# Scores of own and preceding keys in one product, tanh for the first two groups' gates, the first mask on TensorE, and a new order of the work, in a windowed attention followed by a gated MLP

## The chip, the cores and the metric

The kernel runs on one core of one Trainium2 chip. The metric is the device time of one execution in microseconds. A run holds the span from the first to the last instruction and a little around it.

The engines named below are TensorE (PE: matmuls, and PEld: the loading of their stationary operand), VectorE (DVE), ScalarE (ACT), GpSimd (POOL), and SyncE (SP), whose queue and POOL's start the transfers (DMA). SBUF is the on-chip memory, PSUM the memory that matmuls write. Each engine works through its own list of instructions in order.

## What is computed

Attention over 768 positions with a window of 128 and 4 sink positions, for 4 sequences of 8 heads with 64 columns each; its output, 3072 tokens of 512, goes through an MLP of width 2048 with the gate h * sigmoid(1.702 h).

```python
scores = scale * np.matmul(q, k.transpose(0, 1, 3, 2))
keep = is_sink | in_window            # pos < 4, or 0 <= i - j < 128
scores = np.where(keep, scores, -1000000000.0)
scores = scores - np.max(scores, axis=-1, keepdims=True)
a = np.exp(scores)
a = a / (np.sum(a, axis=-1, keepdims=True) + 1e-09)
x = np.matmul(a, v)                   # heads side by side: 3072 x 512
h = x @ w_in                          # 512 x 2048
g = h * (1.0 / (1.0 + np.exp(-1.702 * h)))
out = g @ w_out                       # 2048 x 512
```

## The kernel before

**Blocks and groups.** The tokens are cut into 24 blocks of 128 (b; sequence bb = b // 6, place r = b % 6) for attention and 12 groups of two blocks (g) for the MLP. A block of queries meets its own 128 keys (own), the 128 keys ahead of it (prv, if r > 0) and the four sinks (snk, if r > 0). Since the window is 128 wide, for each query exactly one of a key position's own and preceding key is in the window, so own and preceding scores share one 128-wide tile: where the own key is later than the query, the preceding key's score is put in its place.

**Steps of a block.** POOL starts the loads of q, k and v, which also turn 32 bit floats into 16 bit ones (L253, L257). q and k are transposed to qkT: by TensorE and a copy for blocks 0 to 3 (tq, L336), by a DMA transpose from SP's queue for the others (L349). TensorE makes the scores, 8 products of 64 rows by 128 columns for own and 8 for prv (L374), and the sinks' (L390). VectorE puts prv's scores into own's tile by a predicated copy (L414), or, for r = 0, adds a mask (bias0, L406); takes the maximum of each head (L426, L442, L445), and subtracts it into e, an SBUF tile (L481, L496). ScalarE takes the exponential (a, L513); in blocks 0 to 3, one half is taken straight from PSUM by four activations with a bias (L467, set by nb). The weights a are transposed to at (ta on TensorE and a copy, L552, for blocks 0 to 3; a DMA transpose, L584, for others). POOL splits at by two selections into the part of the preceding keys, atp, and that of its own, at (L516, L520). TensorE multiplies by the values (av; sinks L603, own L609, preceding L613); each values tile has a 65th column of ones that gives the sum of the weights. VectorE divides by it (rcp and xn, L624 and L625; a "norm" below). xn is transposed to xT (tx, L638, and a copy for blocks 0 to 3; a DMA transpose, L649, for others).

**Sink values.** vsb holds the sinks' values of a sequence, 32 rows of 4 sinks x 8 heads, of which each head's columns are kept by a mask (ownm, L301), in a tile of 128 rows that is set to zero first (L235). It is multiplied by a ninth 128-wide piece of at.

**Steps of a group.** hT is made in 8 tiles of 8 matmuls of 128x256 (L669; group 0 is "split": 16 of 128x128, each for one block's tokens, so that it can begin with block 0 alone). ScalarE takes Gelu_apprx_sigmoid of each into gT (L681). Its table is another than the exponential's, so the planner batches the gates of a group, and a table load stands ahead of each change. The second product o takes 16 matmuls of 128x512 for each block, in four quarters (L697); a copy takes it to osb and SP's queue writes it out (L714).

**The order.** All steps are ops of a small planner (class Plan). Each op has an engine or a choice of two, a key (its urgency), a cost, ops it depends on, and PSUM or SBUF tiles that it takes and gives back (Buf, RING: how many of each ring there are). run() goes through time and lets each engine take, of the ops that are ready by its costs, the one with the smallest key; the resulting order is what each engine is given. On the chip each engine keeps that order and waits where something isn't there yet. Loads that aren't in the list `loads` have a time ahead of which the planner doesn't start them (after0, after).

**PSUM** has 8 banks of 2 KB a partition: mm 3 (hT, o, transposes, and the scores of own for blocks 1 and 3), own 2, pv 2 (prv and av), mi 1 (snk).

Of the kernel before, what the change touches and what calls it, by code (L numbers as in the profile page):

```python
# [27 lines left out]
    tq=(0, 1, 2, 3), ta=(0, 1, 2, 3), tx=(0, 1, 2, 3), nb={0: 1, 1: 1, 2: 1, 3: 1}, wide=(1, 3),  # L28
    split=(0,), gbatch=8, after0=25.0, after=8.0,
    loads="q0 k0 q1 k1 v0 v1 i0 i1 q2 k2 q3 k3 i2 i3 v2 v3 o0 o1 o2 o3".split(),  # L30
)
RING = dict(qkn=4, qkt=8, e32=4, a16=4, at=4, atp=4, xn=3, xt=4, gt=3, osb=4, mm=3, own=2, pv=2, mi=1)
# [15 lines left out]
class Op:  # L48
    def __init__(self, eng, key, cost, emit, deps=(), take=(), give=(), table=None, lat=0.2, xfer=0.0, after=0.0, batch=0, xt=False):
        self.eng = eng if isinstance(eng, dict) else {eng: cost}  # L50
        self.key, self.emit = key, emit
        self.deps = [d for d in deps if d is not None]
        self.take, self.give, self.table, self.batch = list(take), list(give), table, batch
        self.lat, self.xfer, self.after, self.xt = lat, xfer, after, xt
        self.start = self.end = self.done = None
        for b in self.give:
            b.left += 1


class Plan:  # L60
# [3 lines left out]
    def __init__(self, rings):  # L64
        self.ops, self.free = [], dict(rings)

    def add(self, *a, **kw):
        op = Op(*a, **kw)
        op.seq = len(self.ops)
# [3 lines left out]
    def _give(self, op):  # L73
        for b in op.give:
            b.left -= 1
            b.t = max(getattr(b, "t", 0.0), op.done)
            if b.left == 0:
                self.gives.append((b.t, b.ring))

    def run(self):  # L80
        t_eng = {e: 1.0 for e in self.ENGINES}
        free, table, batch, now = dict(self.free), "exp", 0, 0.0
        pending, order, self.gives = list(self.ops), [], []
        queue = {POOL: [], SP: []}
        lanes = {POOL: [], SP: []}
        while pending or any(queue.values()):
            for item in [x for x in self.gives if x[0] <= now]:
                self.gives.remove(item)
                free[item[1]] += 1
            for e in self.ENGINES:  # L90
                if t_eng[e] > now:
                    continue
                best = None
                for op in pending:
                    if e not in op.eng or op.after > now:
                        continue
                    if any(d.done is None or d.done > now for d in op.deps):
                        continue
                    need = {}
                    for b in op.take:  # L100
                        need[b.ring] = need.get(b.ring, 0) + 1
                    if any(free[r] < n for r, n in need.items()):
# [3 lines left out]
                    if op.xfer and len(lanes[e]) >= self.LANES:  # L106
                        d = lanes[e][-self.LANES].done
                        if d is None or d > now:
                            continue
                    if best is None or (op.key, op.seq) < (best.key, best.seq):  # L110
                        best = op
                if best is None:
                    continue
                op, cost = best, best.eng[e]
                op.on = e
# [5 lines left out]
                op.start, op.end = now, now + cost  # L121
                t_eng[e] = op.end
                for b in op.take:
                    free[b.ring] -= 1
# [3 lines left out]
                else:  # L128
                    op.done = op.end + op.lat
                    self._give(op)  # L130
                pending.remove(op)
                order.append(op)
            live = [q[0] for q in queue.values() if q and q[0][0].end <= now]
            times = [t for t in t_eng.values() if t > now] + [x[0] for x in self.gives if x[0] > now]
            times += [op.done for op in order[-400:] if op.done is not None and op.done > now]
            times += [op.after for op in pending if op.after > now]
            times += [now + h[1] * len(live) for h in live]
            assert times, [(o.eng, o.key) for o in pending[:20]]
            step = max(min(times), now + 1e-6) - now
# [3 lines left out]
            for h in live:  # L143
                if h[1] <= 1e-6:
                    queue[h[0].on].pop(0)
                    h[0].done = now + (0.6 if h[0].xt else 1.9)
                    self._give(h[0])
# [4 lines left out]
def _consts():  # L152
# [5 lines left out]
    own = np.zeros((32, 2, 4, D1), np.float16)  # L158
    for h in range(8):
        own[4 * h : 4 * h + 4, h % 2, h // 2] = 1.0  # L160
# [5 lines left out]
        own.reshape(32, 8 * D1),  # L166
# [4 lines left out]
def kernel(  # L171
# [39 lines left out]
    ident = const.tile([P, P], FP16, name="ident")  # L211
    later = const.tile([P, P], U16, name="later")
    bias0 = const.tile([P, P], BF16, name="bias0")
    bias1 = const.tile([P, 4], BF16, name="bias1")
    ownm = const.tile([32, 8 * D1], FP16, name="ownm")
# [4 lines left out]
    vsa = const.tile([32, 4, D1], FP32, name="vsa")  # L220
    vsb = const.tile([P, 4, 2, 4, D1], FP16, name="vsb")
# [3 lines left out]
    def hw(key, cost, fn, xfer, **kw):  # L225
# [7 lines left out]

    z_k = plan.add(DVE, -90, 0.2, lambda: nc.vector.memset(ksb, 0.0))
    z_v = plan.add(DVE, -89, 1.2, lambda: nc.vector.memset(vsb, 0.0))  # L235
# [3 lines left out]
        plan.add(DVE, -86 + i, 0.2, lambda i=i: nc.vector.memset(a16s[i][:, 8 * P : 9 * P], 0.0))  # L239
        for i in range(RING["a16"])  # L240
    ]
# [45 lines left out]
    for b in range(NBLK):  # L287
        for w in "qkv":
            if f"{w}{b}" not in ld:
                ld[f"{w}{b}"] = load_block(w, b, -60 + 8 * (b - 4), CFG["after0"] + CFG["after"] * nblk)  # L290
                nblk += w == "v"
    ld_win, ld_wout = [ld[f"i{f}"] for f in range(4)], [ld[f"o{f}"] for f in range(4)]

    o_vsa = [
        hw(-94 + bb, 0.45, lambda bb=bb: nc.sync.dma_start(vsa[:, bb, 0:D], v[bb, :, 0:4, :]), 0.1, deps=[z_s])
        for bb in range(Bsz)
    ]

    def vs_build(bb):
        def go(e):  # L300
            (nc.vector if e == DVE else nc.gpsimd).tensor_tensor(  # L301
                out=vsb[0:32, bb].rearrange("p l j d -> p (l j) d"),
                in0=vsa[:, bb].unsqueeze(1).to_broadcast((32, 8, D1)),
                in1=ownm.rearrange("p (n d) -> p n d", d=D1),
                op=ALU.mult,
            )

        return plan.add({DVE: 0.45, POOL: 0.8}, 48 * bb - 41, 0, go, deps=[o_vsa[bb], z_v, o_own])

    o_vsb = [vs_build(bb) for bb in range(Bsz)]  # L310

    def copy(e, dst, src):
        if e == DVE:
            nc.vector.tensor_copy(out=dst, in_=src)
        else:
# [3 lines left out]
    qkt = [sb("qkt", (P, 8, P), FP16, f"qkT{b}") for b in range(NBLK)]  # L319
    xt = [sb("xt", (P, 4, 2 * P), FP16, f"xT{g}") for g in range(NG)]  # L320
    o_qkt, o_ks, o_own_s, o_x = {}, {}, {}, {}

    for b in range(NBLK):
        bb, r = divmod(b, 6)
        g, i = divmod(b, 2)
        K0 = 8 * b
        nb = CFG["nb"].get(b, 0)


        if b in CFG["tq"]:  # L330
            tp = ps("mm", (P, 8, P), FP16, f"tq{b}")

            def t_qk(b=b, g=g, i=i, tp=tp):
# [5 lines left out]
                PE, K0 - 48, 0.55, t_qk, deps=[ld[f"q{b}"], ld[f"k{b}"], o_ident], take=[tp],  # L339
# [3 lines left out]
                {DVE: 0.65, ACT: 1.05}, K0 - 48, 0,  # L343
                lambda e, b=b, tp=tp: copy(e, qkt[b](), tp()), deps=[a], take=[qkt[b]], give=[tp],
            )
        else:

            def t_qk(b=b, g=g, i=i):
                nc.sync.dma_start_transpose(qkt[b](), qkn[g]()[:, i].rearrange("p w h d -> p (w h d)"))  # L349

            o_qkt[b] = plan.add(
                SP, K0 - 48, 1.25, t_qk, deps=[ld[f"q{b}"], ld[f"k{b}"]], take=[qkt[b]], give=[qkn[g]], xfer=1.26, xt=True
            )
        if r == 0:

            def sink_keys(b=b, bb=bb):
# [400 lines left out]
```

## Time and profile before

| what | us |
| --- | --- |
| median of 3 runs (252.06 to 254.63) | 253.05 |
| profiled execution | 252.76 |
| its span, first to last instruction | 251.0 |
| the first hT tile of group 0 starts at | 25.14 |
| the first hT tile of group 1 starts at | 58.97 |
| the last copy osb starts at | 247.11 |
| 12 + 12 table loads of 1.28 each | 30.8 |

The mean granted clock of TensorE was 0.976. The largest groups of the profile:

```profile
L669 PE MATMUL hT<-xT,w_in 128*128 128x256 f16 (+1 forms) x832 | 94.1, 268 | 3.8 <-ACT xT L316 1.3
L697 PE MATMUL o<-w_out,gT 128*128 128x512 f16 x384 | 86.2, 379 | 0.0
L681 ACT ACTIVATE gT<-hT 128x512 f16<-128x512 f32 x96 | 57.0, 597 | 45.3 <-PE hT L669 45.1
L414 DVE COPY_PREDICATED own<-later,prv 128x512 f32<-128x512 uint16 x40 | 25.9, 691 | 36.7 <-PE prv L374 29.0
L426 DVE TENSOR_REDUCE mx<-own 128x4 f32<-128x512 f32 x48 | 31.2, 681 | 0.1
```

A row is: line, engine, operation, tiles (output <- inputs), partitions x elements and type, count | busy us, mean ns of one | idle time of the engine just ahead of them, and what ended most of it. A matmul's mean is longer than the distance to the next, since they are pipelined: 8 of 128x256 take 0.87 us in a dense stretch, 4 of 128x512 take 0.87 as well. The page has four DMA rows that matter below:

```profile
w_out<-in_moe_w_out_dram POOLq DMA_DIRECT2D x4, 512.0 KB, 14.1
qkT<-qkn SPq DMA_TRANSPOSE x20, 4.9
at<-a SPq DMA_TRANSPOSE x20, 3.3
xT<-xn SPq DMA_TRANSPOSE x20, 5.7
```

The last number is the median time from issue to landing.

### The profile page before, as it was taken

The numbers are of one execution on the slowest core, as the hardware profiler recorded it, in microseconds if no ns is written. First come the engines' busy times: TensorE is split into PE (matmuls) and PEld (weight loads), VectorE is DVE, ScalarE is ACT, GpSimd is POOL, SyncE is SP. The second block draws the span as 40 slices with busy tenths as digits, with TensorE's granted clock in tenths as the row PEclk, the third lists the DMA queues.
The fourth block names the chain that finished last, engine by engine and source line by source line (L and its number), as shares of the span: only waits on it lengthen the run. The fifth ranks groups of instructions, "written<-read, shape, count | busy, mean of one in ns | idle before, by whom it ended". The sixth has DMA issues, their size and how long they took to land.

```text
span 251.0 us, 5308 instructions
## 1 busy us (share of the span) xinstructions
PE 217.1 (86%) x2123; PEld 148.1 (59%) x2123; DVE 133.7 (53%) x332; ACT 136.9 (55%) x198; POOL 113.5 (45%) x130
## 2 busy tenths in 40 slices
PE   0528787857998989998999996999999999999993
PEld 0306655434764845946747845848669477594851
DVE  4596920496687356964866556749647663010000
ACT  2326576825473474586466654657765666471621
POOL 8955832387471904904916807719055060210000
PEclk9999999985899999999999999999999999999998
DMA  9999999995999998999999999999999343320202
GB/s 77 167 175 193 206 188 151 156 129 82 136 110 190 169 149 201 101 117 202 156 159 231 127 111 215 110 175 182 119 253 130 71 131 44 74 77 3 84 0 84
DMA packets 138663, 34.09 MB, mean 136 GB/s; under 512 B 131440, under 2 KB 135568, under 8 KB 138640
## 3 DMA queue, kind: packets, MB, share of 16 engines
q0 software_dynamic: 79104, 13.64, 81.9%
q1 hardware_dynamic: 59536, 20.13, 44.0%
q8 instruction: 16, 0.26, 0.4%
q14 instruction: 7, 0.06, 0.1%
HBM read 27.43 MB, written 6.29 MB: 134 GB/s over the span
## 4 chain that ended last, share of the span: by engine, by line
PE 60%; DMA 20%; DVE 12%; issue 2%; POOL 2%; SPq 1%; ACT 1%; POOLq 0%; ACTq 0%; DVEq 0%
PE hT L669 27%; PE o L697 22%; DMA qkT<-qkn 8%; DMA qkn<-in_k_dram 5%; DMA at<-a 2%; DVE own L414 2%; PE own L374 2%; DMA xT<-xn 2%; DVE xn L625 2%; DVE mx L426 2%; DMA vsa<-in_v_dram 2%; PE av L609 2%; PE av L613 1%; DVE e L481 1%; PE prv L374 1%
## 5 line engine op out<-in xcount | busy, mean ns | idle before, releaser
L669 PE MATMUL hT<-xT,w_in 128*128 128x256 f16 (+1 forms) x832 | 94.1, 268 | 3.8 <-ACT xT L316 1.3
L697 PE MATMUL o<-w_out,gT 128*128 128x512 f16 x384 | 86.2, 379 | 0.0
L669 PEld LDWEIGHTS <-w_in 128*128 128x128 f16 x832 | 75.0, 99 | 14.6 <-issue 3.2
L681 ACT ACTIVATE gT<-hT 128x512 f16<-128x512 f32 x96 | 57.0, 597 | 45.3 <-PE hT L669 45.1
L516 POOL TENSOR_SCALAR_AFFINE_SELECT atp<-at 128x1024 f16<-128x1024 f16 (+1 forms) x23 | 22.5, 976 | 95.3 <-DMA at<-a 73.3
L697 PEld LDWEIGHTS <-gT 128*128 128x128 f16 x384 | 36.5, 98 | 41.0
L414 DVE COPY_PREDICATED own<-later,prv 128x512 f32<-128x512 uint16 x40 | 25.9, 691 | 36.7 <-PE prv L374 29.0
L426 DVE TENSOR_REDUCE mx<-own 128x4 f32<-128x512 f32 x48 | 31.2, 681 | 0.1
L316 ACT COPY osb<-o 128x512 f32<-128x512 f32 x23 | 13.5, 585 | 30.4 <-PE o L697 27.3
L513 ACT ACTIVATE a<-e 128x1056 f16<-128x1056 f32 (+3 forms) x27 | 24.3, 919 | 10.4 <-issue 8.8
L481 DVE TENSOR_TENSOR e<-own,mx 128x512 f32<-128x512 f32 x44 | 28.8, 683 | 1.2
L253 POOL DMA_DIRECT2D v<-in_v_dram x24 | 21.7, 906 | 4.6 <-DMA w_in<-in_moe_w_in_dram 3.0
L520 POOL TENSOR_SCALAR_AFFINE_SELECT at<-at 128x1024 f16<-128x1024 f16 (+1 forms) x23 | 22.4, 972 | 1.6
L257 POOL DMA_DIRECT2D qkn<-in_q_dram x24 | 21.9, 912 | 2.4 <-DMA w_out<-in_moe_w_out_dram 1.6
L257 POOL DMA_DIRECT2D qkn<-in_k_dram x24 | 21.7, 905 | 1.8 <-DMA w_out<-in_moe_w_out_dram 1.7
L625 DVE TENSOR_TENSOR xn<-av,rcp 128x256 f16<-128x256 f32 x48 | 20.4, 424 | 1.6
L609 PE MATMUL av<-v,at 128*128 128x65 f16 x192 | 17.5, 198 | 3.1 <-POOL at L520 2.9
L624 DVE RECIPROCAL rcp<-av 128x4 f32<-128x4 f32 x48 | 8.4, 174 | 21.6 <-PE av L613 20.0
L609 PEld LDWEIGHTS <-at 128*128 128x128 f16 x192 | 14.5, 100 | 5.9 <-POOL at L520 4.9
L374 PEld LDWEIGHTS <-qkT 64*128 64x128 f16 x352 | 11.0, 99 | 11.7 <-issue 6.4
L681 ACT ACT_TABLE_LOAD x12 | 15.4, 1283 | 0.2
L613 PE MATMUL av<-v,atp 128*128 128x65 f16 x160 | 15.3, 196 | 0.0
(43 smaller groups left out, 135.7 us busy)
## 6 DMA issues: line engine op xcount, KB each, us to landing
out_dram<-osb SPq DMA_DIRECT2D x24, 256.0 KB, 2.4
qkn<-in_q_dram POOLq DMA_DIRECT2D x24, 128.0 KB, 4.8
qkn<-in_k_dram POOLq DMA_DIRECT2D x24, 128.0 KB, 6.1
v<-in_v_dram POOLq DMA_DIRECT2D x24, 128.0 KB, 6.6
w_in<-in_moe_w_in_dram POOLq DMA_DIRECT2D x4, 512.0 KB, 10.3
w_out<-in_moe_w_out_dram POOLq DMA_DIRECT2D x4, 512.0 KB, 14.1
qkT<-qkn SPq DMA_TRANSPOSE x20, 4.9
at<-a SPq DMA_TRANSPOSE x20, 3.3
```

Source lines behind the costliest of these rows:

```text
L257: key, 0.88, lambda: nc.gpsimd.dma_start(buf()[:, i, w], src), 0.87,
L414: nc.vector.copy_predicated(out=own[l](), mask=later.unsqueeze(1).to_broadcast((P, 4, P)), data=prv[l]())
L426: lambda l=l, own=own, small=small: nc.vector.tensor_reduce(out=small[:, l], in_=own[l](), axis=AX.X, op=ALU.max),
L481: nc.vector.tensor_tensor(out=e32()[:, 512 * l : 512 * l + 512].rearrange("p (j s) -> p j s", j=4), in0=own[l](), in1=small[:, l].unsqueez ...
L513: nc.scalar.activation(out=a16()[:, lo:hi], in_=e32()[:, lo:hi], func=AF.Exp, scale=scale)
L516: nc.gpsimd.affine_select(out=atp()[:, lo : lo + n], in_=at()[:, lo : lo + n], pattern=[[0, n], [-1, P]], compare_op=ALU.is_gt, fill=0.0, ...
L520: nc.gpsimd.affine_select(out=at()[:, lo : lo + n], in_=at()[:, lo : lo + n], pattern=[[0, n], [1, P]], compare_op=ALU.is_ge, fill=0.0, ba ...
L609: nc.tensor.matmul(av()[:, j], at()[:, c], v65[:, b, h], start=(r == 0), stop=(r == 0))
L625: nc.vector.tensor_tensor(out=xn().rearrange("p (j l) d -> p l j d", l=2)[:, l], in0=av()[:, :, 0:D], in1=rcp.unsqueeze(2).to_broadcast((P ...
L669: nc.tensor.matmul(ht()[:, n], w_in16[:, c, bass.ts(f, P)], xt[g]()[:, c, tok], start=(c == 0), stop=(c == 3))
L681: lambda fs=fs, tok=tok, gt=gt, ht=ht: nc.scalar.activation(out=gt()[:, fs[0] : fs[-1] + 1, tok], in_=ht(), func=AF.Gelu_apprx_sigmoid),
L697: nc.tensor.matmul(po(), gt()[:, F, bass.ts(t, P)], w_out16[:, F], start=(F == 0), stop=(F == NF - 1))
```

## The change

- **Scores.** The transposed queries and keys of a sequence's six blocks lie in one tile, qs (128 x 6 x 8 x 128, two of them), so a block's keys and its predecessor's lie one behind the other and one product of 256 columns gives both. The score tile sc (two banks, two of them) holds two pairs of heads for preceding and own keys; a block has two such halves (u = 0, 1: heads 0 to 3 and 4 to 7), and maxima, subtractions and norms go by these halves. The predicated copy reads and writes the same tile.
- **First mask.** For r = 0 the mask is added by TensorE: per half two products of identb (the identity in bfloat16) with bias0, 256 columns each, ahead of the score products, which accumulate on it. The VectorE adds go.
- **Sinks.** Their scores snk are copied to an SBUF tile ss (VectorE or ScalarE; for r = 1 with the mask). vsb has 48 rows (0 to 15 for heads 0 to 3, 32 to 47 for 4 to 7); the product takes 16 rows. vsa is loaded by 8 transfers instead of 4. The large memset goes; small ones for e come.
- **Exponentials.** nb is empty: in all blocks both halves go through e on VectorE.
- **Gates of groups 0 and 1.** tanh(0.851 h) on ScalarE into th (32 bit, SBUF), then (th + 1) * h on VectorE into gT, which is twice the gate; the factor 0.5 goes into the copy of o to osb. Tanh is planned as of the exponential's table.
- **PSUM.** mm 3, sc 2 x 2, av 1 (values and snk).
- **Order.** q, k and v of blocks 4 and 5 are in the list `loads`; the planner's costs are new; and each op's key is replaced by a number of the list KEYS (some 1010 numbers), a permutation. An engine's order within the program so differs throughout: hT tiles, o quarters and halves of blocks come interleaved, and hT tiles of two groups too.

The core of the diff:

```diff
-    tq=(0, 1, 2, 3), ta=(0, 1, 2, 3), tx=(0, 1, 2, 3), nb={0: 1, 1: 1, 2: 1, 3: 1}, wide=(1, 3),
-    split=(0,), gbatch=8, after0=25.0, after=8.0,
-    loads="q0 k0 q1 k1 v0 v1 i0 i1 q2 k2 q3 k3 i2 i3 v2 v3 o0 o1 o2 o3".split(),
...
+    nb={},
...
+    tanh=(0, 1),
...
+    loads="q0 k0 q1 k1 v0 v1 i0 i1 q2 k2 q3 k3 i2 i3 v2 v3 q4 k4 q5 k5 o0 o1 o2 o3 v4 v5".split(),
...
-RING = dict(qkn=4, qkt=8, e32=4, a16=4, at=4, atp=4, xn=3, xt=4, gt=3, osb=4, mm=3, own=2, pv=2, mi=1)
+RING = dict(qkn=4, qs=2, e32=4, a16=4, at=4, atp=4, xn=3, xt=4, gt=3, osb=4, th=2, mm=3, sc=2, av=1)
...
+    def sink_values(bb):
+        def load(u):
+            nc.sync.dma_start(vsa[32 * u : 32 * u + 16, bb, 0:D], v[bb, 4 * u : 4 * u + 4, 0:4, :])
...
+        sc = [ps("sc", (P, 2, 2, 2, P), FP32, f"sc{b}_{u}") for u in range(2)]
+
+        def scores(u, bb=bb, r=r, sc=sc):
+            t = sc[u]()
+            if r == 0:
+                for l in range(2):
+                    nc.tensor.matmul(
+                        t[:, l, :, 1], identb, bias0.unsqueeze(1).to_broadcast((P, 2, P)), start=True, stop=False
+                    )
+            for jj in range(2):
+                for l in range(2):
+                    rows, j = slice(64 * l, 64 * l + 64), 2 * u + jj
+                    if r == 0:
+                        nc.tensor.matmul(
+                            t[:, l, jj, 1], qs[bb]()[rows, r, j], qs[bb]()[rows, r, 4 + j], start=False, stop=jj == 1
+                        )
+                    else:
+                        nc.tensor.matmul(
+                            t[:, l, jj], qs[bb]()[rows, r, j], qs[bb]()[rows, r - 1 : r + 1, 4 + j],
+                            start=True, stop=True,
+                        )
...
+                    nc.vector.copy_predicated(
+                        out=t[:, :, 1], mask=later.unsqueeze(1).to_broadcast((P, 4, P)), data=t[:, :, 0]
+                    )
...
                 if r > 0:
+                    rows = slice(32 * u, 32 * u + 16)
                     nc.tensor.matmul(
-                        av().rearrange("p j d -> p (j d)"), at()[:, 8],
-                        vsb[:, bb, l].rearrange("p j d -> p (j d)"), start=True, stop=False,
+                        av().rearrange("p n d -> p (n d)"), at()[rows, 8],
+                        vsb[rows, bb].rearrange("p n d -> p (n d)"), start=True, stop=False,
                     )
...
+            if g in CFG["tanh"]:
+                th = sb("th", (P, 4 * P), FP32, f"th{g}_{u}")
...
+                        out=th(), in_=ht().rearrange("p f t -> p (f t)"), func=AF.Tanh, scale=0.851
...
+                    lambda fs=fs, tok=tok, gt=gt, ht=ht, th=th: nc.vector.scalar_tensor_tensor(
+                        out=gt()[:, fs[0] : fs[-1] + 1, tok], in0=th().rearrange("p (f t) -> p f t", f=len(fs)),
+                        scalar=1.0, in1=ht(), op0=ALU.add, op1=ALU.mult,
+                    ),
...
+    if KEYS:
+        for op, key in zip(plan.ops, KEYS):
+            op.key = key
     order = plan.run()
```

## The prediction

> **What bounds the kernel now.** I read the page first, then the order of the matmuls and the idle time ahead of them on TensorE, then the other engines where TensorE was thin, then windows with the granted clock, then the landing times of the transposes.
>
> The page, engines and slices (one digit is 6.3 us):
>
> ```profile
> span 251.0 us, 5308 instructions
> ...
> PE 217.1 (86%) x2123; PEld 148.1 (59%) x2123; DVE 133.7 (53%) x332; ACT 136.9 (55%) x198; POOL 113.5 (45%) x130
> ...
> PE   0528787857998989998999996999999999999993
> ```
>
> TensorE is full from the tenth digit on; what is lost lies in the first 59 us. The first 8-matmul hT tile of group 1 starts at 58.97, the last o matmul ends at 247.1: 188.1 us in which only TensorE sets the pace. Up to 58.97 it is fed by attention of blocks 0 to 5 and by group 0. The timelines of VectorE and ScalarE say why that takes so long:
>
> ```profile
> 33.08 0.18 DVE L496 TENSOR_TENSOR e<-snk,mx 128x32 f32<-128x32 f32 x1
> 47.30 0.56 DVE L314 COPY at<-ta 128x512 f16<-128x512 f16 x2 [14.04 <-PE ta L552]
> ...
> 36.78 1.28 ACT L681 ACT_TABLE_LOAD   x1
> ...
> 44.13 1.28 ACT L513 ACT_TABLE_LOAD   x1
> 45.43 0.75 ACT L513 ACTIVATE a<-e 128x512 f16<-128x512 f32 x2
> ```
>
> VectorE stands 14.04 us for the transposed weights of blocks 2 and 3: their scores are ready at 33.1, but ScalarE holds the gate table until group 0 is through and takes the exponentials only at 45.4. The windows then show the clock:
>
> ```profile
> 56.00:59.00 3.00, 0.99 (x12) 0.67 (x10) 2.86 (x9) 0.58 (x1) 1.09 (x1) 0.50 0.87 165
> 59.00:62.00 3.00, 3.00 (x29) 1.99 (x29) 0.94 (x3) 2.53 (x3) 2.99 (x4) 0.50 0.12 10
> ```
>
> The columns are window, length, busy PE, PEld, DVE, ACT, POOL, granted clock, DMA share, GB/s. After the thin stretch the clock is at 0.50, and stays so to about 64.7: of 5.7 us of dense work half, 2.85 us, is lost.
>
> **The sum's base.** The profiled execution took 252.76 us, 1.76 outside its span of 251.0; it lies 0.3 below the median of the runs, 253.05. All terms below are against 252.76.
>
> **Group 1 starts earlier.** In the changed program group 0 and 1 take tanh, which follows exponentials with no table load between (table loads fall from 24 to 16), so blocks 2 and 3 no longer wait for the gates. What is then next is VectorE. From the first maximum of block 0 to the last xn of block 3 its order holds 40 operations of 128x512 (12 maxima, 10 selections, 10 subtractions, 8 tanh gates), 8 norms and some 40 small ones. In dense stretches of the trace a large one follows the next after 0.60 us (two selections at 24.91, the next at 26.10), a norm takes 0.55, small ones 0.1 to 0.35: 24.0 + 4.4 + 6.7 = 35.1 us. The gate reads an SBUF and a PSUM operand of 512 floats; its nearest row is the subtraction, so 0.60. The chain begins at 11.2 instead of 14.0: the two bias adds (1.30) are gone from VectorE and the small loads of sink values, of which the last lands at 11.3 now, are split among the maxima. That gives 46.3 if VectorE never waits. I add 4: block 4's scores need its transposed queries. Now 46 units of 131 KB (14 loads of q, k and v, 8 weight loads of four units) land between 4.3 and 38.9, 0.75 each; in the new order of POOL's queue 36 units stand up to the last query of blocks 4 and 5, so it lands at about 31, and a transpose took 3.0 to 7.5; and three o quarters (0.87 each) stand ahead of block 5's scores on TensorE. With tx and the xT copy (0.4 + 0.6) group 1 starts at 51.0, bounds 47.2 (no wait) and 55 (the transpose at 7.5 and one more such wait): **-8.0** (-11.8 to -4.0).
>
> **Clock.** In the new stretch from 23 to 51 TensorE has about 18 us of work in 28 (before: 5 in the 12 us ahead of 59). I take the clock as held: **-2.85**, or 0 if not (251.3 in the end): between 47 and 59 no gap on TensorE was above 1.34 us and yet the clock fell, so thin work is enough, and the new stretch is only twice as dense. The Trainium skill ("TensorE: Matmul & The Clock Gate", Part 1) lets the clock fall only after an idle window of about 3.4 us. By that rule the loss would not return; the trace does not agree with it, and decides.
>
> **TensorE's own work after that.** One o quarter of group 0 now stands behind the first hT of group 1: **+0.9**. The mask by TensorE is 16 products of 256 columns; 12 of them, for blocks 6, 12 and 18, fall in the dense part, at 0.109 each (hT row, 0.87 for 8): **+1.3**; what it takes off VectorE there (6 adds of 0.6) lies beside it and gives nothing. The merged score product halves the matmuls but not their columns: 8 x 128 now take 0.33 as own and 0.22 as prv just behind it; 8 x 256 as two halves take 0.44 plus what own pays for coming after other work, 0.11, once or twice: 0.55 to 0.66 against 0.55, or less by the saved issues. I take 0, bounds -1.5 and +1.7 for 15 blocks. The sink values' product takes 16 rows instead of 128 in each of 34 dense halves; no row shows it. It costs nothing if like the 128-row product (0.11 for 260 columns, no gap), 0.11 if like a change to 64 rows, 0.22 if it pays on the way back as well: 0 to 7.5. The rest of the half keeps 128 rows, so I take 0.05: **+1.7**. The Trainium skill ("TensorEngine Tiling (Array Packing)", Key Properties) says that a change of tiling mode drains the engine, which speaks against this part; at own's 0.11 each half it would make 250.4 in place of 248.4, within the forecast's band.
>
> **New waits in the dense part.** Before, from 58.97 on, 88 hT tiles and 88 o quarters at 0.87 and 25 us of attention make 178.3 us of work; 188.1 - 178.3 - 2.85 leaves 7.0 of waits and switches. Among these only one is for xT:
>
> ```profile
> 73.38 5.65 DMA xT<-xn
> 79.07 1.05 PE hT L669 x8
> ```
>
> From group 3 on the old order leaves 9.7 to 14.4 us of TensorE work between a group's last values product and its first hT. The new order, counted in the same units (hT tile 0.87, o quarter 0.87, score half 0.22, sinks 0.19, values half 0.36), leaves 4.7, 6.2, 6.6, 3.6, 5.8, 6.2, 5.8 for groups 2 to 8, 13.2 for 9, 4.3 and 4.4 for the last two. Group 5, for one: two hT, one o quarter, one values half, two score halves, sinks. The hand-over needs a norm (0.66 from matmul to xn), 0.1, the transpose and 0.05:
>
> ```profile
> DMA to landing us min/median/max: 2.4/5.7/8.4
> ```
>
> At the median that is 6.5, and 1.8 + 0.3 + 0 + 2.9 + 0.7 + 0.3 + 0.7 = 6.7 us are uncovered; the last two groups run after the loads, where it landed in 2.4 to 3.5, and are covered. TensorE waits in order, so all that is queued behind that hT waits too. A single bank for values and sinks, and shorter ways from scores to values (8.5 to 14.3 us of other work for six of blocks 4 to 10, before 10.8 to 24.3; one values half waited 2.1 for POOL, one 1.1 and one 0.9 us went to transposed queries), I put at 3: together 9.7 in place of 7.0, **+2.7**. Bounds: 2.7 (all covered but these) and far above, below.
>
> Costed at nothing, since TensorE is the bound: 16 tanh gates' second pass on VectorE (group 1 with blocks 6 and 7 needs about 15 of 17 us there; without that cover 0.6 each), half-wise maxima, sink copies, eight small loads on SP's queue (0.7 each, done before block 4's transposes), the factor 0.5 in osb's copy, fewer table loads.
>
> Sum: -8.0 - 2.85 + 0.9 + 1.3 + 1.7 + 2.7 = -4.3, so **248.4**.
>
> **Rivals.**
> Covers hold: the transposes, issued singly, land near 3 as the late ones do; waits fall from 9.7 to about 2.7: 241.4. For it: 2.4 to 3.5 late. Against: none that I could resolve between 70 and 185 landed under 5.4.
> The gain is spent: the hand-over takes the mean of those (5.8, 5.6, 7.0, 7.2, 8.4, 5.7, 6.0, 5.4, 5.4, 8.1: 6.5); each of seven groups loses 0.8 more, 253.9; or the clock falls again, 251.3.
> Slower: the hand-over of xT becomes the bound at seven groups. At the upper half of those rows (7.7) uncovered time is 20.6 instead of 6.7: 262.3. It decides from a mean landing of 6.7, where waits pass 255.6. For it: the mean is close. Against: half of the rows are at 5.4 to 5.8.
> That the merged product saves TensorE time is not in the sum at all: equal columns.
>
> **Numbers.** Forecast 0.38 (244 to 250.5), covers hold 0.20 (below 244), gain spent 0.24, slower 0.18. A measurement here tells about 1% from no change (250.5 to 255.6): faster 0.58, same 0.24, slower 0.18. Range 241 to 258, leaving about 0.1 at each end; it takes in the bounds of the start and of the 16-row product.
>
> **What will show it.** VectorE without a 14 us gap and group 1's first hT near 51; granted clock 1.00 around 50 to 65; xT waits ahead of the first hT of groups 2, 5 and 6, near 2, 3 and 1 us; values halves still 0.36 to 0.41; 16 table loads. Wrong if group 1 starts after 55, or if TensorE waits more than 15 us after it.

## The result and the profile after

| | before | changed |
| --- | --- | --- |
| median us (range; runs) | 253.49 (252.06 to 254.63; 4) | 260.69 (260.38 to 261.03; 4) |
| profiled execution; its span | 252.76; 251.0 | 261.03; 259.3 |
| mean granted clock | 0.976 | 0.974 |
| first hT of group 0; of group 1 | 25.14; 58.97 | 23.73; 53.71 |
| last product starts | 246.65 | 254.44 |

The ratio is 1.0287, interval 1.0229 to 1.0345: slower, outside the range of the prediction. (Now and then a run is disturbed by a lower clock; ratios here leave such runs out and medians don't, so the two can differ, and one kernel below has no ratio.) The page of the changed kernel, engines, slices of 6.5 us and clock:

```profile
span 259.3 us, 5051 instructions
...
PE 230.3 (89%) x1979; PEld 142.9 (55%) x1979; DVE 149.6 (58%) x394; ACT 125.1 (48%) x184; POOL 113.8 (44%) x130
...
PE   0559695999959999999699999997999999999993
...
PEclk9999996799989999999979999999999999999999
```

TensorE is fuller than before (89% for 86%), with fewer matmuls, and yet later. The 14.04 us for which VectorE stood are gone: ScalarE takes tanh and exponentials in turn, with no table load between them. Its timeline:

```profile
32.80 0.60 ACT L765 ACTIVATE th<-hT 128x512 f32<-128x512 f32 x1 [1.14 <-PE hT L751]
33.92 0.78 ACT L600 ACTIVATE a<-e 128x512 f16<-128x512 f32 x2 [0.53 <-DVE e L562]
34.60 0.58 ACT L765 ACTIVATE th<-hT 128x512 f32<-128x512 f32 x1
```

What took the place of that gap is in TensorE's timeline and in the windows (columns as in the prediction, the clock third from the end):

```profile
41.78 0.27 PE L470 MATMUL snk<-ksb,qs 128*128 128x8 f16 x4 [2.60 <-DMA qs<-qkn]
...
43.71 4.94 PE L797 MATMUL o<-w_out,gT 128*128 128x512 f16 x12
48.48 0.24 PE L470 MATMUL snk<-ksb,qs 128*128 128x8 f16 x4
```

```profile
36.00:40.00 4.00, 2.84 (x45) 2.42 (x42) 2.75 (x7) 2.87 (x6) 2.82 (x5) 1.00 1.55 136
40.00:44.00 4.00, 2.22 (x22) 1.29 (x23) 1.91 (x4) 0.19 (x1) 2.93 (x4) 0.66 1.36 179
44.00:47.00 3.00, 3.00 (x8) 1.06 (x7) 2.97 (x11) 0.00 (x0) 0.86 (x2) 0.50 1.98 163
47.00:50.00 3.00, 3.00 (x19) 1.17 (x19) 1.23 (x4) 1.20 (x2) 0.29 (x1) 0.81 2.43 155
```

TensorE waits 2.60 us for block 4's transposed queries; then the clock is at half, and 12 o products take 4.77 us, which is 2.60 at 0.217 each.

**Where the time went.** From group 1's first hT to the last product I took, for every matmul, the distance to the start of the next, and set against it what its shape has in dense stretches (0.217 us for 512 columns on 128 rows, 0.109 for 256, half as much on 64 rows, where two run side by side). What is above that is a change of row count, a half clock (the distance doubled), or a wait (over 0.18).

| us | before | changed | difference |
| --- | --- | --- | --- |
| group 1's first hT at | 58.97 | 53.71 | -5.3 |
| products by their shapes | 173.9 | 175.9 | +2.0 |
| changes to 16 rows and back | 0 | 6.9 | +6.9 |
| changes to 64 rows and back | 4.1 | 6.3 | +2.2 |
| waits | 6.8 | 7.9 | +1.1 |
| half clock | 2.7 | 3.2 | +0.5 |
| rest | 0.1 | 0.3 | +0.2 |

With 0.5 more behind the last product's start this is the 8.3 us of the spans within 0.2. The largest term can be read in the timelines. A values half of the kernel before, then of the changed one:

```profile
101.82 1.04 PE L669 MATMUL hT<-xT,w_in 128*128 128x256 f16 x8
102.69 0.27 PE L603 MATMUL av<-vsb,at 128*128 128x260 f16 x1
102.80 0.19 PE L609 MATMUL av<-v,at 128*128 128x65 f16 x1
...
103.05 1.04 PE L669 MATMUL hT<-xT,w_in 128*128 128x256 f16 x8
```

```profile
97.76 0.49 PE L751 MATMUL hT<-xT,w_in 128*128 128x256 f16 x3
98.18 0.28 PE L688 MATMUL av<-vsb,at 16*128 16x260 f16 x1
98.39 0.20 PE L694 MATMUL av<-v,at 128*128 128x65 f16 x1
...
98.65 1.91 PE L751 MATMUL hT<-xT,w_in 128*128 128x256 f16 x16
```

Starts count, not lengths. Before, 8 hT take 0.87 and the product of 260 columns 0.11. After, 3 hT take 0.42 (0.33 by shape) ahead of the 16 rows, and the same 260 columns 0.21: about 0.10 going in and 0.10 coming out, and a half that is 0.47 long in place of 0.36.

### The profile page after: what moved, and what is told of

It reads as the page before. It is cut to its first block, busy times and chain, and to the rows that moved or that the text cites. A ratio compares the mean times of both kernels' runs of the same rounds, so it can differ in the third digit from the quotient of the medians.

```text
span 259.3 us, 5051 instructions
## 1 busy us (share of the span) xinstructions
PE 230.3 (89%) x1979; PEld 142.9 (55%) x1979; DVE 149.6 (58%) x394; ACT 125.1 (48%) x184; POOL 113.8 (44%) x130
## 4 chain that ended last, share of the span: by engine, by line
PE 67%; DMA 20%; POOL 7%; DVE 1%; ACT 1%; SPq 1%; issue 1%; POOLq 0%; ACTq 0%
PE o L797 28%; PE hT L751 28%; DMA qs<-qkn 6%; DMA qkn<-in_q_dram 6%; DMA xT<-xn 5%; POOL qkn L315 3%; PE sc L451 3%; PE av L694 3%; DMA at<-a 3%; PE av L688 2%; PE av L696 1%; POOL v L311 1%; POOL w_in L324 1%; POOL atp L603 1%; SPq L668 1%
## 5 line engine op out<-in xcount | busy, mean ns | idle before, releaser
L797 PE MATMUL o<-w_out,gT 128*128 128x512 f16 x384 | 94.6, 391 | 0.0
L781 ACT ACTIVATE gT<-hT 128x512 f16<-128x512 f32 x80 | 47.2, 597 | 39.0 <-PE hT L751 38.8
L511 DVE COPY_PREDICATED sc<-later,sc 128x512 f32<-128x512 uint16 x40 | 27.0, 690 | 16.8 <-PE sc L451 16.7
L600 ACT ACTIVATE a<-e 128x1088 f16<-128x1088 f32 (+3 forms) x31 | 27.2, 896 | 11.8 <-DVE e L562 7.0
L520 DVE TENSOR_REDUCE mx<-sc 128x4 f32<-128x512 f32 x48 | 32.2, 685 | 0.8 <-PE sc L447 0.4
L562 DVE TENSOR_TENSOR e<-sc,mx 128x512 f32<-128x512 f32 x48 | 32.3, 686 | 0.5
L382 ACT COPY osb<-o 128x512 f32<-128x512 f32 x18 | 10.6, 586 | 31.6 <-PE o L797 26.1
L451 PE MATMUL sc<-qs 64*128 64x256 f16 x160 | 15.9, 293 | 7.0 <-DVE e L562 5.5
L694 PEld LDWEIGHTS <-at 128*128 128x128 f16 x192 | 12.8, 99 | 8.0 <-DVE ss L478 1.5
L765 ACT ACTIVATE th<-hT 128x512 f32<-128x512 f32 x16 | 9.5, 594 | 13.4 <-PE hT L751 13.2
```

Of the source, the lines that this page charges most:

```text
L451: nc.tensor.matmul(t[:, l, jj], qs[bb]()[rows, r, j], qs[bb]()[rows, r - 1 : r + 1, 4 + j], start=True, stop=True,)
L511: nc.vector.copy_predicated(out=t[:, :, 1], mask=later.unsqueeze(1).to_broadcast((P, 4, P)), data=t[:, :, 0])
L520: lambda u=u, sc=sc, small=small: nc.vector.tensor_reduce(out=small[:, u], in_=sc[u]().rearrange("p l j w s -> p (l j) w s")[:, :, 1], axi ...
L562: nc.vector.tensor_tensor(out=e32()[:, 512 * u : 512 * u + 512].rearrange("p (j l s) -> p l j s", l=2, s=P), in0=sc[u]()[:, :, :, 1], in1= ...
L600: nc.scalar.activation(out=a16()[:, lo:hi], in_=e32()[:, lo:hi], func=AF.Exp, scale=scale)
L694: nc.tensor.matmul(av()[:, n], at()[:, h], v65[:, b, h], start=(r == 0), stop=(r == 0))
```

## The experiments

Ratios are to the kernel before on the same chip.

**The price of a row count.** The changed kernel with 128 rows, and the kernel before with 32:

```diff
-    vsb = const.tile([48, 4, 4, D1], FP16, name="vsb")
+    vsb = const.tile([P, 4, 2, 4, D1], FP16, name="vsb")
...
-                        av().rearrange("p n d -> p (n d)"), at()[rows, 8],
-                        vsb[rows, bb].rearrange("p n d -> p (n d)"), start=True, stop=False,
+                        av().rearrange("p n d -> p (n d)"), at()[:, 8],
+                        vsb[:, bb, u].rearrange("p n d -> p (n d)"), start=True, stop=False,
```

> The changed kernel with one thing altered: the sink product works on all 128 rows of the transposed weights against a table of own values that is zero outside its 16 rows, so that no product on 16 rows is left on TensorE; two builds of 16 rows per sequence replace one of 48. The output stays the reference's. Theory A (each change of the row count costs TensorE about 0.1 us, into the 16 rows and out of them, and 6.9 us of the changed kernel's trace are that): 34 halves lose about 0.2 us each, so the time falls from 260.7 to about 254 (252 to 256); in the trace the distances at the sink products lose their extra 0.1 us on either side. Rival B (the 0.1 us are waits of TensorE for the transposed weights that fall at the same place, or the loss lies in the order): the time stays at 259.5 to 261.5 and the idle time moves to another instruction. Where the expected time is missed upwards, rival C: the saved time is taken up by new waits for xT or for score tiles, which the list of waits would show.

```diff
-                        av().rearrange("p j d -> p (j d)"), at()[:, 8],
-                        vsb[:, bb, l].rearrange("p j d -> p (j d)"), start=True, stop=False,
+                        av().rearrange("p j d -> p (j d)"), at()[0:32, 8],
+                        vsb[0:32, bb, l].rearrange("p j d -> p (j d)"), start=True, stop=False,
```

> The kernel before with one thing altered: its sink product works on the 32 rows that hold own keys instead of on all 128; the output stays the reference's, and the order of instructions is the same. Theory A: a sink product on fewer rows costs about 0.1 us going in and 0.1 us going out, so 40 of them add 6 to 8 us: about 260 (257 to 262). Rival B (a product on few rows costs what its columns cost): the time stays within 1 us of the kernel before, 252 to 254.5.

Measured: 258.83 (254.8 to 260.55), ratio 1.0114 (0.9997 to 1.0231), so about 1.7% or 4.4 us below the changed kernel's ratio (its interval is wide and meets the changed kernel's; the medians differ by 1.9, the profiled spans by 3.4); and 257.16 (255.49 to 257.95), ratio 1.0143 (1.0069 to 1.0217). The second kernel's timeline has the same half as above:

```profile
103.53 1.03 PE L669 MATMUL hT<-xT,w_in 128*128 128x256 f16 x8
104.49 0.28 PE L603 MATMUL av<-vsb,at 32*128 32x260 f16 x1
104.71 0.20 PE L609 MATMUL av<-v,at 128*128 128x65 f16 x1
...
104.96 1.03 PE L669 MATMUL hT<-xT,w_in 128*128 128x256 f16 x8
```

0.96 for 0.87 ahead of it, 0.22 for 0.11, 0.47 for 0.36, by this one edit: 34 halves pay 3.3 going in (0.097 each) and 3.4 coming out (0.101). Theory A holds for the price; rival B falls in the trace. But 6.7 us more in the kernel before cost 3.6 us of time. In its profiled run the part from group 1 on took only 1.0 more, with 5.1 us less of waits (1.7 for 6.8) and 1.0 less of half clock, while group 1 came 3.7 later (62.64), with the clock low ahead of it. And 6.2 us less in the changed one (6.9, less 0.7 that score halves then pay on their way back) gave 4.4, with 4.4 more of waits (12.3 for 7.9). Block 0's first maximum came later there, at 13.83 in place of 12.40, but group 1 1.1 earlier, at 52.58, so it is not the start that took the gain. Rival C took part of it. The longest wait, in the chain of waits of the run with 128 rows:

```profile
124.28 0.43 DVE xn L711
124.71 0.02 issue
124.73 7.09 DMA xT<-xn
131.82 0.04 issue
131.86 1.14 PE hT L756 x9
```

In the changed kernel the same hand-over reads:

```profile
123.54 0.44 DVE xn L706
123.98 0.02 issue
123.99 6.03 DMA xT<-xn
130.03 0.04 issue
130.07 2.08 PE hT L751 x9
```

TensorE's work that covers it, from the last values product ahead of it to the wait, is the same in both within 0.1 us (4.1 and 4.2). What grew is the landing, from 6.03 to 7.09; why is open.

**What tanh is worth.** In the kernel before, with its own way of ordering:

```diff
-    split=(0,), gbatch=8, after0=25.0, after=8.0,
+    split=(0,), tanh=(0, 1), gbatch=8, after0=25.0, after=8.0,
```

> The kernel before with one part of the change alone: the gates of groups 0 and 1 by tanh (one ACT operation with the exponential's table and one on VectorE, the factor 0.5 at the output copies), everything else and its way of ordering as before. The output stays the reference's. Theory A (the 14 us gap ahead of group 1 came from the gate table's batch, and its end is worth what group 1 gains): group 1's first hT moves from 58.97 to 51 to 54, the end follows by 4 to 6 us: 247 to 250. Rival B (what group 1 gains is spent in later waits, for xT and q, k tiles, as in the changed kernel where the waits rose by 1.1 us and half-clock time by 1.2): 251 to 254. Slower than 254.6 would mean that the two extra operations per gate on VectorE and ACT are late for someone.

Measured: 256.71 (255.69 to 258.12), ratio 1.0137 (1.0064 to 1.0211). Both theories were too low; the time lies in the expectation's last branch, over 254.6. TensorE's timeline from the end of group 1 on:

```profile
67.37 0.40 PE L378 MATMUL own<-qkT 64*128 64x128 f16 x8
...
74.52 0.23 PE L378 MATMUL prv<-qkT,qkT 64*128 64x128 f16 x1 [0.74 <-DMA qkT<-qkn]
...
76.88 0.26 PE L378 MATMUL own<-qkT 64*128 64x128 f16 x1 [1.52 <-DVE e L485]
...
84.64 1.67 PE L673 MATMUL hT<-xT,w_in 128*128 128x256 f16 x7 [1.29 <-DMA xT<-xn]
```

Group 1 began at 51.02, as theory A had it, and is through its last o product at 71.4. Then there is nothing but attention until group 2's first hT at 84.64, which in the kernel before came at 79.07. From 78 to 86 the clock was at 0.50. MLP work that is done early is missing later as cover: that is one reading. The other is the expectation's, that the gates' second pass comes late for someone: VectorE was busy 13.1 of the 16 us from 70 to 86, and the wait at 76.88 ends on its subtraction. No run parts the two.

**The start of the changed kernel.** The searched order has the builds of all four sequences' vsb in VectorE's first microseconds; it stood for their loads until 9.79 us, and block 0's first maximum came at 12.40. They were moved to where they are needed:

```diff
     order = plan.run()
+    for build, op in zip(o_vsb, behind):
+        build.on = DVE
+        order.remove(build)
+        order.insert(order.index(op) + 1, build)
```

> The changed kernel with one thing moved: the four builds of the own values vsb (one per sequence) stand on VectorE directly behind the last subtraction of their own sequence's second block, in place of the first microseconds, where the searched order had them with those of sequences 2 and 3 ahead of block 0's first maximum; every other instruction keeps its place. The output stays the reference's. Theory C (part of the gain at the start is lost because VectorE stands until 9.79 and 10.89 us for the loads of vsa of sequences that are needed only after 100 us): block 0's first maximum moves from 12.40 to about 9.5, the first hT from 23.7 to about 21, group 1 from 53.7 to 51, and the time falls by 2 to 3 us to 258 to 259. Rival D (the start is bound by the loads of block 4's queries and keys, whose transposition landed at 41.7 us): all moves until then, but TensorE then waits longer for that landing, group 1 stays at 53 to 54 and the time at 260 to 261.

> The changed kernel with both: the sink product on 128 rows, and the builds of vsb moved to the second block of their sequence. (The run with 128 rows alone had its builds in the first microseconds too, twice as many, and a clearing of 1.8 us ahead of them, so that block 0's first maximum came 1.4 us later than in the changed kernel: part of its gain was hidden by that.) The output stays the reference's. Theory A: the 6.9 us at the changes to 16 rows go, less the 0.7 us that the score halves then pay for the way back, less what comes back as waits for transposes (4.4 us more in the run with 128 rows alone): 255 to 257. If theory C holds for the start, 2 us less still. Rival D: no lower than the run with 128 rows alone, 258 to 259.

Measured: 264.44, ratio 1.0499 (1.0418 to 1.0581), and 263.58 (259.46 to 265.07) without a ratio. In the first, the maximum came at 9.55 and group 0's first hT at 21.90, as theory C had it, but group 1's only at 52.61, nearer to rival D's 53 to 54 than to theory C's 51; and the time rose by 4 us by the medians and 5 by the ratios, which none expected. Why is open. The second lies above both of its ranges and tells nothing apart.

**The order.** The changed kernel with the formula's keys, and with score halves side by side. In the second and in all orders below, the planner's run is replaced by a list:

```diff
-    if KEYS:
+    if False:
```

> The changed kernel without its searched order: the operations go out by the formula's keys, with the same planner, tiles and operations. The output stays the reference's. Theory A (what the changed kernel loses lies in its products' row counts): the excess at changes of row count stays, since any order with the same halves has about as many of them, and the time is no lower than the changed kernel's: 261 to 270, by how much the search had saved in waits. Rival B (the searched order is what makes it slow on the chip, since it was fitted to the planner's costs): 253 to 258.

```diff
-    order = plan.run()
+    order = []
+    for word in ORDER:
+        op = plan.ops[int(word[1:])]
+        op.on = dict(P=PE, A=ACT, D=DVE, G=POOL, S=SP)[word[0]]
+        order.append(op)
```

> The changed kernel with one thing moved on TensorE: in 14 blocks the two halves of the scores stand directly behind one another, where the searched order had two to nineteen other steps between them; the other engines keep their orders. The output stays the reference's. Theory E (each stay in 64 rows costs about 0.10 us going in and 0.14 us coming out): 14 stays fewer, 3.3 us less in the distances at changes of row count, and the time falls by 1 to 3 us, to 258 to 260, as far as no new wait for a score tile takes it up. Rival F (the halves' extra time is not the change of rows): the distances stay and the time is 260 to 262.

Measured: 269.46, ratio 1.0593 (1.0484 to 1.0701); and 261.60 (260.72 to 263.21), ratio 1.0416 (1.0343 to 1.0489). The search is no loss: without it the kernel is 8 to 9 us slower. With halves paired, the changes of row count fell by 1.8 us in the dense part (8 stays fewer there), the waits rose by 3.1 (10.9 for 7.9), and nothing was gained: theory E holds for the distances and not for the time.

**The loads.** A third of the later loads taken away, in both kernels, and then with the row counts changed as well:

```diff
-            return sw(key, 0.88, lambda: nc.gpsimd.dma_start(v65[:, b, :, 0:D], src), 0.85, deps=[z_1], after=after)
+            return sw(key, 0.88, lambda: nc.gpsimd.dma_start(v65[:, b, :, 0:D], src) if b < 6 else None, 0.85, deps=[z_1], after=after)
```

(and v65[:, b % 6] in the products)

> The changed kernel with the loads of the values left out from block 6 on; the products of those blocks read the values of the first sequence's block of the same place, so the output of sequences 1 to 3 is not the reference's. Order and everything else as in the changed kernel; the loads' bytes of the later blocks fall by a third, and GpSimd issues 18 loads less. Theory H (TensorE's waits are the landings of the transposes qs, at and xT, which share the DMA engines with the loads, 5.7, 4.2 and 2.5 us in the median): the medians fall by about a quarter, TensorE's waits from 7.9 to 2 to 4 us, and the time to 254 to 257. Rival I (the transposes are late for other reasons: the queue that issues them, or the steps before them): the landings stay within 0.3 us and the time at 259 to 261.

> The kernel before with the loads of the values left out from block 6 on, its products reading the first sequence's values, as was done with the changed kernel (which fell from 260.7 to 253.3 us): the output of sequences 1 to 3 is not the reference's. Theory L (the loads burden both kernels alike, so the 7 us between them are TensorE's own work): the kernel before falls as far, to 245 to 248. Rival M (the kernel before hardly waits for transposes; the burden of the loads is the changed kernel's loss): it falls by 3 us or less, to 250 to 253, and the two kernels end within 3 us of each other.

> The changed kernel with both edits: the sink product on 128 rows, and the loads of the values left out from block 6 on (the products read the first sequence's values, so sequences 1 to 3 are not the reference's). Theory N (the 0.1 us at a change of row count reach the end in full where the loads do not decide when the transposes land): 6.2 us (6.9 less 0.7) below the 253.3 us of the changed kernel without these loads, plus up to 1.4 us of its later start: 246.5 to 249. Rival O (the waits take up the gain here too, as they did with the loads in place, where 6.2 us gave 1.9): 250.5 to 253.

> The kernel before with both edits: the sink product on 32 rows, and the loads of the values left out from block 6 on (sequences 1 to 3 are not the reference's). Theory N: 6 to 8 us above the 248.0 us of the kernel before without these loads: 254 to 256. Rival O (half of it is taken from waits, as with the loads in place, where 6.7 us cost 3.5): 250 to 252.5.

| without the later v loads | median us | ratio (interval) |
| --- | --- | --- |
| changed | 253.32 | 1.0004 (0.9956 to 1.0052) |
| changed, 128 rows | 251.29 | 0.9927 (0.9880 to 0.9974) |
| before | 247.96 | 0.9829 (0.9768 to 0.9890) |
| before, 32 rows | 255.04 | 1.0084 (1.0036 to 1.0133) |

The clock and the transposes of the first, from its page:

```profile
PEclk9999999999999999999999999999999999999999
...
qs<-qkn SPq DMA_TRANSPOSE x20, 4.8
at<-a SPq DMA_TRANSPOSE x20, 3.3
```

They landed in 5.7 and 4.2 us before the edit. The changed kernel falls by 7.4 us: its start by 2.4 (group 1 at 51.26; some of this may be chance, since most of what was left out comes later), the half clock from 3.2 to nothing, the waits by 1.9. Theory H holds for the landings of qs and at (xT stayed at 2.5); the waits fell less and the clock gave more than it said. The kernel before falls by about 5, so of the 7.2 us between the two medians 5.4 stay: theory L, mostly.

The last pair answers how far a row count reaches. In the kernel before, where one wait of 0.7 us is left, just ahead of group 1, and hardly one behind it, 34 halves on 32 rows cost 7.1 us by the medians, against 6.7 in the trace: theory N, the price in full. In the changed kernel 128 rows give 2.0, though the trace has 6.2 less: rival O. Its chain of waits shows where it went:

```profile
117.21 0.43 DVE xn L711
117.64 0.02 issue
117.66 6.76 DMA xT<-xn
124.42 0.04 issue
124.46 1.57 PE hT L756 x9
```

It is the hand-over of the same group, with the later loads of v gone. What TensorE saves is waited for (3.75 us at that point, 1.47 with 16 rows), and paid again at a lower clock (1.6 us, none with 16 rows). TensorE's cover is again the same within 0.1 us (4.1 and 4.2); the landing is not, 6.76 us against 4.59 with 16 rows (from 118.73). With 128 rows the transpose goes out 1.1 us earlier and lands 1.1 us later. It starts at 117.66, just as POOL begins to issue the last of three loads of q and k; with 16 rows it starts 1.6 us behind that load's start. So the faster TensorE here brought the transpose closer to the loads; that it lands later for that reason fits, but no run parts it from other causes.

**Orders by measured prices.** The same planner was given what the traces show (transposes 1.35 times as long and 1.2 us later, a change of rows 0.095 and 0.142) and searched again:

> The changed kernel with the sink product on 128 rows and with its order searched once more, by the same planner with prices as the traces have them: a transposition on the DMA queues 1.35 times as long as planned and landing 1.2 us later, the loads of vsa landing 5.5 us after they are issued, a stay of TensorE in 64 rows 0.095 us going in and 0.142 us coming out. The output stays the reference's. Theory J (beside the 16 rows, the changed kernel loses by an order fitted to prices that were too low): PE's waits fall from the 12.3 us of the run with 128 rows alone to 4 to 7, and the time to 251 to 254. Rival K (no order helps, since the score halves and the DMA queues bind any order): 257 to 259, as the run with 128 rows alone.

> The kernel before with its order searched by the same planner with the same measured prices; nothing else changed, and the output stays the reference's. Theory J: the kernel before gains less by it than the changed kernel, since its order was not fitted to the planner's prices beyond the formula: 250 to 252. Rival K: 252.5 to 255, no gain.

> The kernel before with its order searched by the planner with measured prices, as in the run b1_before_order, but with the first 12 us of the load queues and the first 7 us of the engines left as they were (in that run the search had put a load of weights ahead of block 0's queries, so that TensorE began at 8.5 us in place of 5.1), and with a price for TensorE's half clock after a wait of over 1.8 us. The output stays the reference's. Theory J: TensorE begins at 5.1 us again and the time is 247.5 to 250.5, below both kernels. Rival K: 251.5 to 254, the order has nothing left to give.

> The changed kernel with the sink product on 128 rows and its order searched in the same way, with the start left as it was (in the run e10_rows128_order TensorE began at 8.6 us, for the identity's load). The output stays the reference's. Theory J: 251 to 255, by the start alone 3.4 us below that run's 258.1. Rival K: 256 to 259. If it stays above 250 while the kernel before with its order searched goes below, the tiles of the changed kernel (score halves of 64 rows, the mask on TensorE) are what keeps it behind, whatever the order.

> The order of b1_before_order (the kernel before, searched with measured prices) with one thing put back: the first two blocks' queries and keys are loaded first, ahead of the weights that the search had put there. The output stays the reference's. Theory J: the 3.4 us that TensorE began later in that run (8.5 in place of 5.1 us) come off its 252.2: 248 to 250, below both kernels. Rival K: what is won at the start is lost before group 1 to the weights that now come later: 251.5 to 253.

> The order of e10_rows128_order (the changed kernel with its sink product on 128 rows, searched with measured prices) with one thing put back: the identity is loaded first, so that TensorE begins at 5.1 us in place of 8.6. The output stays the reference's. Theory J: 254 to 256 (258.1 less up to 3.4). Rival K: 257 to 259, the start is bound by the loads and not by that.

> The kernel before with the gates of groups 0 and 1 by tanh, as in the run e3_before_tanh (256.7), and its order searched by the planner with measured prices, the start left as it was. The output stays the reference's. Theory J (what tanh loses in the order of before, where TensorE runs out of work ahead of group 2, is a matter of order): 249 to 252. Rival K (group 1's gain can't be kept, since group 2's scores wait for the loads of blocks 4 and 5 whatever the order): 254 to 257.

| kernel | median us | ratio (interval) |
| --- | --- | --- |
| e10_rows128_order | 258.14 | 1.0179 (1.0096 to 1.0262) |
| e11_rows128_order2 | 261.45 | 1.0331 (1.0257 to 1.0406) |
| e12_rows128_order3 | 258.48 | 1.0242 (1.0172 to 1.0313) |
| b1_before_order | 252.18 | 0.9958 (0.9914 to 1.0002) |
| b3_before_order2 | 251.25 | 0.9969 (0.9929 to 1.0008) |
| b5_before_order3 | 251.92 | 0.9996 (0.9955 to 1.0037) |
| b4_before_tanh_order | 254.39 | 1.0034 (0.9978 to 1.0090) |

Rival K nearly throughout (b1_before_order and b3_before_order2 fall between the two forecasts, e11_rows128_order2 above both). No order searched again for the changed tiles came below the 1.0114 of e1_rows128, and none of the kernel before is told apart from it. In b5_before_order3 TensorE began 3.4 us earlier than in b1_before_order and yet group 1 came 1.2 us later, at 59.35 in place of 58.12. The weights went out later too (the first of w_in at 4.91 in place of 1.31, the last of w_out at 20.96 in place of 19.38), which fits a start that is bound by the loads together, not by one of them. Tanh, with an order of its own, gains nothing over the same kernel without it: b4_before_tanh_order is 3 us above b3_before_order2 by the medians and 1.6 by the ratios, whose intervals overlap. So no version beats the kernel before by more than a measurement tells.

## Why the prediction was wrong

- **The sink product on 16 rows: the step that failed.** The prediction had bounds of 0 and 0.22 for each half and took 0.05, "the rest of the half keeps 128 rows": +1.7. It measures 0.20, 6.9 in all, since the rest of the half, just because it keeps 128 rows, pays the way back. The direction was right, the size four times too small; with 0.20 alone the sum is 253.6, and the gain is gone. The Trainium skill ("TensorEngine Tiling (Array Packing)", Key Properties) says that a change of tiling mode drains the engine. The traces agree, 0.10 us each way; the prediction weighed it at 0.11 a half, for one way only.
- **Merged scores, taken at 0, bounds -1.5 to +1.7:** +2.2, outside them. There are 31 entries into 64 rows for 21 (30 and 18 of them free of waits and the half clock, as counted in the table), each about 0.09 in and 0.14 out, because the halves go out singly and come between other work.
- **The start, -8.0:** -5.3. The gates' gap closed, with 16 table loads, as said. But the transpose of block 4's queries, issued at 31.86, landed at 41.74: 9.9 us, where the prediction's bound was 7.5. The half clock behind that wait took 2.2 more. (The prediction's own addends, 46.3 + 4 + 0.4 + 0.6, make 51.3 and not 51.0.)
- **The clock, -2.85:** +0.5. The 2.7 of before went, but 3.2 were lost at other places, behind waits for qs and xT.
- **The o quarter and the mask, +2.2:** +2.0, right.
- **The waits, 9.7 in place of 7.0:** 7.9 in place of 6.8. xT landed in 2.5 us in the median, as in "covers hold"; only groups 2 and 5 waited for it, 0.9 and 2.8, of the 6.7 that the prediction gave to xT. Most of the rest are two waits for transposed queries and keys, 2.0 and 1.5. So the total came near 9.7 in part by luck.

The misses, 5.2 + 2.2 + 2.7 + 3.4 - 0.2 - 1.6, make 11.7 of the 12.6 us between 248.4 and 261.03. The rival that ended slower had the right sign by another way: xT decides at one group of seven. The price of the row change is shown by its own edits in both kernels; how the rest of the loss divides between the score halves, the mask and tanh rests on the trace's distances, since no run takes one of these alone out of the changed kernel.

## What to carry to other kernels

A product on fewer rows saves no columns and costs a change of row count on each side: with 34 of them, 0.2 us each, that was more than the whole gain that was forecast; between products on 128 rows, filling the rows with zeros is cheaper. A gap closed at the start is worth only what no later wait takes back: ask which loads are next there, and what will cover the later stage when its work has been done early. A search of the order gave 8 to 9 us over the planner's own here, but searching again with measured prices gave nothing more. Where two bounds lie close together (here TensorE and the hand-over through transposes), relieving one shows as waits at the other, and the time of the transposes is itself not fixed: ask what a faster engine brings them closer to.

## What was not expected of the hardware

- A change from 128 rows to 64, 32 or 16 costs 0.093 to 0.097 us. Back from 16 or 32 it costs 0.101; back from 64, 0.121 behind products of 128 columns and 0.142 behind those of 256.
- A wait can be paid twice. After the changed kernel's wait of 2.8 us, from 127.3 to 130.07, the clock was at 0.57 for the next 4 us; the kernel before waited 2.27 us at 152 and kept 1.00. The Trainium skill ("TensorE: Matmul & The Clock Gate", Part 1) puts the idle window at about 3.4 us; the traces here have the clock fall after less (the waits of 2.60 and 2.8), and they decide.
- With the later loads of v gone, two kinds of transposes of the changed kernel, on the other queue, landed 0.9 us sooner in the median (qs 5.7 to 4.8, at 4.2 to 3.3), and xT no sooner (2.5). In the kernel before, qkT gained 1.5 (4.9 to 3.4), xT 0.6 (5.7 to 5.1) and at 0.1 (3.3 to 3.2).
